# A delta-rule attention and two MoE layers on one core: the first triangular inverse cut into blocks of 16, a second room for step 1, and a new order of the program

## The chip, the cores and the metric

The kernel runs on one core of a Trainium2 chip. The metric is the device time of one execution in microseconds (us), from the first to the last instruction with the small frame around it; lower is better.

The engines by the names of the profile: PE is TensorE (matmuls; PEld its weight loads), DVE is VectorE, ACT is ScalarE, POOL is GpSimd, SP is SyncE, which here issues nearly all DMAs. Each engine works through its own instructions strictly in the order of the program; engines wait for each other by semaphores.

## The reference

Inputs are q, k, v of 4 batches x 8 heads x 768 tokens x 48 and a beta for each token. Cut to what matters:

```python
# attention: a state of 48x48 per head, updated token by token (delta rule)
k_n = k / (norm(k) + 1e-6)
for t in range(768):
    y[t]  = q[t] @ state
    state = state + beta[t] * outer(k_n[t], v[t] - k_n[t] @ state)
# first MoE-like layer: x is y as 3072 tokens x 384
h = x @ w_in                      # 384 -> 2048
x = (h * sigmoid(h)) @ w_out      # 2048 -> 384
# second: 8 experts, soft routing P by 8 rounds of row and column scaling
P = balance(exp(x @ w_gate))
out = sum over e of P[:, e] * (relu(x @ w1[e]) @ w2[e])   # 384 -> 1024 -> 384
```

w_in and w_out arrive as 64-bit floats; the kernel splits them on the chip into a high and a low 32-bit part.

## The kernel before, in words

**Attention in 12 steps of 64 tokens.** The recurrence inside a step is replaced by the inverse of a 64x64 unit lower triangular matrix per head (32 heads, in two groups `bp` of 16). `gram_k` / `gram_kq` compute the products of the keys on PE (psum `gk`, `gkq`), they are written to DRAM (`nd`) and read back by `units` so that 128 small 32x32 triangles (2 steps x 2 halves x 32 heads) lie one per partition in the tile `nu`. `tri(j, prio)` inverts these 128 triangles for the steps 2j and 2j+1 on DVE: square roots and scales (`root_act`, `d_`), a scale of `nu`, then for each of 31 columns `t` a multiply (L607, into `tmpu`) and an add (L605, into `tu`), and a last scale of `tu` (L620, kept as `O["td2", j]`). In `tri(0)` most columns are cut into two row ranges, so that two chains of instructions alternate. ACT copies `tu` into `nu` with the two inner axes turned (L623); SP writes `nu` to DRAM as `rd` (L628) and `tu` as `td` (L637).

**Step s.** `rt_load(s)` reads `rd` into the tile `rt` (L647) and `td` and `nd` into the tile `td11`. There is one `rt` and one `td11` for all steps, so the loads of step s wait until step s-1 has used them (`O["u1", s-1, bp]`, `O["z1", s-1]`, `O["r1", s-1]`). `merge(s)` joins the two 32-blocks of each head into the 64-block: 64 small matmuls (`z`, L665), two ACT evacuations (L671), 64 matmuls (`r`, L678), two ACT evacuations (L686). Then, for both `bp`: `state_read` (PE `c`, from step 1 on, then DVE `wq`, L702), `update` (PE `d`, L716, two ACT evacuations), `output` (PE `y` and `s`, and the DVE add of `s` to the state `xs`, L752) and `turn` (PE transposes `t`, ACT and DVE writing `x`, the input of the first MoE layer).

**First MoE layer.** Six blocks of two steps; block b needs the turns of steps 2b and 2b+1. For each of 16 slices f of the hidden layer there is `moe_h` (9 matmuls, L791, then ACT sigmoid, DVE multiply L801, ACT, POOL) and `moe_o` (9 matmuls, L833). They are issued between the attention steps of later blocks.

**Weight sets.** `weight` turns w_in and w_out into two parts: one load (L920), two ACT copies and seven DVE operations (L945 to L956). There are 8 sets `p` of two slices (w_in and w_out); set p is loaded into the place where set p+1 will be built. These DVE operations run before and during block 0, between all other DVE work.

**Second layer.** 64 units of 15 products (L1264) and 12 outputs (L1352), from about 690 us to the end.

**Order of the program.** Nothing is scheduled at run time. Each piece of work is added with `op(engine, cost, fn, deps, prio, ...)`; `Order.emit` is a list planner that runs once, when the program is built. It keeps an estimated time of each engine and of the DMA queue, takes at each step the piece that can start first (within a small window `NEAR` the one with the highest priority) and so fixes the order of each engine's instructions. Priorities are the `prio` arguments plus a table `NUDGE`; `ALT` is a bonus for alternating between two kinds of PE work. Before the first `moe_h` the planner fills idle PE time with dummy matmuls (`idle`, psum `idle`, L1454).

Of the kernel before, what the change touches and what calls it, by code (L numbers as in the profile page):

```python
# [10 lines left out]
F32 = mybir.dt.float32  # L11
# [3 lines left out]
AF = mybir.ActivationFunctionType  # L15
# [26 lines left out]
ALT = 12.4  # L42
# [4 lines left out]
NEAR_PE = 0.14  # L47
NEAR_DVE = 0.0
NEAR_ACT = 0.25
NEAR_POOL = 0.19  # L50

NUDGE = {
    ('ACT', '<lambda>', -15.5): -9.0, ('ACT', '<lambda>', -7.5): -4.8, ('ACT', '<lambda>', 20): 2.1, ('ACT', 'adma', 30): 3.1,
    ('ACT', 'gram_k.ev', 30): 6.7, ('ACT', 'gram_kq', 4.5): 0.1, ('ACT', 'merge', 0.5): 5.5, ('ACT', 'merge', 16): 2.6, ('ACT', 'merge', 2): -2.7,
    ('ACT', 'merge', 20.5): 1.5, ('ACT', 'merge', 22): -0.7, ('ACT', 'merge', 36): -1.8, ('ACT', 'merge', 5.5): 0.9, ('ACT', 'merge', 7): -2.1,
    ('ACT', 'moe_h.hi', 12): -6.7, ('ACT', 'moe_h.sig', 29.5): -0.8, ('ACT', 'norms.sq', -11): 1.0, ('ACT', 'output.ev', 13): 0.8,
    ('ACT', 'outputs', 4.5): 2.0, ('ACT', 'products.evac', 2): 9.1, ('ACT', 'root_act', 4): -11.5, ('ACT', 'rt_load', 32.5): -7.0,
    ('ACT', 'sinkhorn', 3.5): 0.1, ('ACT', 'step_out.cp', -3.5): 12.6, ('ACT', 'step_out.hi', 20): 3.4, ('ACT', 'tokens.parts', -3.5): 0.7,
    ('ACT', 'tri', 15.5): 3.4, ('ACT', 'turn.hi', 15): 0.1, ('ACT', 'units.go', 20): -3.3, ('ACT', 'update', 9): -1.2,
    ('ACT', 'weight.absolute', -4): -1.9, ('ACT', 'weight.hi', 7.5): 1.4, ('ACT', 'weights.hi', -0.5): 1.3, ('DVE', '<lambda>', 17.5): -5.6,  # L60
    ('DVE', '<lambda>', 40): -0.6, ('DVE', 'gram_k.ev', 30): 1.1, ('DVE', 'gram_q', 31): 0.3, ('DVE', 'mask_q', 6): 9.8,
    ('DVE', 'moe_h.mul', 18): 0.5, ('DVE', 'norms', 11): -6.1, ('DVE', 'output.add', 8): 7.6, ('DVE', 'outputs', 4.5): 21.1,
    ('DVE', 'products.add', -3.5): 16.4, ('DVE', 'root_act', 5): 1.1, ('DVE', 'root_act', 8): 4.0, ('DVE', 'root_act.fin', 5): -0.4,
# [22 lines left out]
}  # L86

TINY_HI = float(np.uint32(0x38000000).view(np.float32))


# [1412 lines left out]
```

## Time and profile before

| what | value |
|---|---|
| time, median of 3 runs | 2177.32 us (2176.47 to 2178.69) |
| the profiled execution's own time | 2183.14 us |
| span of that execution, first to last instruction | 2181.3 us |
| PE busy | 2148.3 us, 98% of the span |
| DVE busy | 1741.8 us, 80% |
| POOL busy | 1539.6 us, 71% |
| ACT busy | 1021.5 us, 47% |

The profile shows one execution. A share of busy time is an average over stages that have different limits, and a busy PE can still be at half clock or running dummy matmuls, so each stage is read by itself. [...] The DMA share is the mean busy share of the core's 16 DMA engines.

### The profile page before, as it was taken

The numbers are of one execution on the slowest core, as the hardware profiler recorded it, in microseconds if no ns is written. First come the engines' busy times: TensorE is split into PE (matmuls) and PEld (weight loads), VectorE is DVE, ScalarE is ACT, GpSimd is POOL, SyncE is SP. The second block draws the span as 40 slices with busy tenths as digits, with TensorE's granted clock in tenths as the row PEclk, the third lists the DMA queues.
The fourth block names the chain that finished last, engine by engine and source line by source line (L and its number), as shares of the span: only waits on it lengthen the run. The fifth ranks groups of instructions, "written<-read, shape, count | busy, mean of one in ns | idle before, by whom it ended". The sixth has DMA issues, their size and how long they took to land.

```text
span 2181.3 us, 40538 instructions
## 1 busy us (share of the span) xinstructions
PE 2148.3 (98%) x15814; PEld 1912.0 (88%) x15814; DVE 1741.8 (80%) x2999; ACT 1021.5 (47%) x1766; POOL 1539.6 (71%) x1387
## 2 busy tenths in 40 slices
PE   8999999999999999999999999999999999999999
PEld 7888888887877889999999999989999999999998
DVE  6888757557445988888888888888888888888887
ACT  2445343433444554545445445555444454454443
POOL 0143555645376988987888878878888878888784
PEclk9899999999999999999999999999999999999999
DMA  8876342533221101011111110120111101101111
GB/s 248 205 216 158 86 94 62 120 49 89 45 81 73 37 30 37 31 40 33 37 31 36 37 37 31 36 66 30 37 37 37 36 30 37 37 30 37 37 33 48
DMA packets 127424, 136.79 MB, mean 63 GB/s; under 512 B 83392, under 2 KB 91328, under 8 KB 127232
## 3 DMA queue, kind: packets, MB, share of 16 engines
q1 hardware_dynamic: 124864, 133.55, 21.9%
q8 instruction: 124, 2.03, 0.4%
q10 hardware_dynamic: 2368, 0.66, 0.2%
q14 instruction: 68, 0.56, 0.1%
HBM read 108.47 MB, written 25.69 MB: 62 GB/s over the span
## 4 chain that ended last, share of the span: by engine, by line
PE 82%; DVE 6%; DMA 5%; POOL 3%; ACT 1%; SPq 1%; issue 1%; DVEq 0%; POOLq 0%; ACTq 0%
PE o L1352 36%; PE p L1264 29%; PE x2p L833 5%; PE h L791 4%; PE d L716 1%; DVE s L1073 1%; DMA kqp<-gd 1%; PE gkq L456 1%; DMA ke<-in_kq 1%; DVE tmpu L607 1%; PE idle L1454 1%; PE y L731 1%; POOL g L809 1%; DVE tu L605 1%; DVE sg L801 1%
## 5 line engine op out<-in xcount | busy, mean ns | idle before, releaser
L1352 PE MATMUL o<-wb,room 128*128 128x384 f32 x2784 | 792.2, 337 | 3.9 <-POOL room L1073 2.4
L1264 PE MATMUL p<-room,wa 128*128 128x512 f32 x2880 | 732.4, 395 | 0.7 <-DVE x L856 0.7
L1264 PEld LDWEIGHTS p<-room,wa 128*128 128x128 f32 x2880 | 536.7, 189 | 92.9 <-DVE x L856 0.8
L1352 PE MATMUL o<-wb,h 128*128 128x384 f32 x1824 | 609.5, 336 | 0.2 <-ACT room L1212 0.2
L1073 DVE TENSOR_TENSOR s<-s,p 128x512 f32<-128x512 f32 x704 | 477.3, 684 | 92.7 <-PE p L1264 55.9
L1352 PEld LDWEIGHTS o<-wb,room 128*128 128x128 f32 x2784 | 512.3, 188 | 26.2 <-POOL room L1073 3.0
L1368 DVE SCALAR_TENSOR_TENSOR acc<-o,pr,acc 128x384 f32<-128x384 f32 x708 | 429.1, 614 | 83.2 <-PE o L1352 82.9
L1073 POOL TENSOR_TENSOR room<-s,room 128x512 fp32r<-128x512 f32 x232 | 305.6, 1320 | 152.9 <-ACT s L1298 146.7
L1073 POOL TENSOR_TENSOR wa<-wraw,wa 128x640 fp32r<-128x640 f32 x189 | 319.5, 1691 | 52.4 <-ACT wa L1167 50.0
L1352 PEld LDWEIGHTS o<-wb,h 128*128 128x128 f32 x1824 | 342.8, 188 | 14.1 <-ACT s L1298 0.6
L1073 POOL TENSOR_TENSOR wraw<-wraw 128x256 f32<-128x256 f32 x378 | 284.5, 761 | 11.2 <-DMA wraw<-in_w 1.9
L809 POOL TENSOR_TENSOR g<-sg,g 128x512 fp32r<-128x512 f32 x96 | 132.8, 1383 | 209.2 <-ACT g L805 197.4
L1167 ACT ACTIVATE wa<-wraw 128x640 fp32r<-128x640 f32 x189 | 138.9, 735 | 244.0 <-POOL wraw L1073 132.6
L1298 ACT ACTIVATE s<-s 128x512 f32<-128x512 f32 x384 | 242.3, 631 | 10.3
L1073 DVE TENSOR_TENSOR s<-p,s 128x512 f32<-128x512 f32 x320 | 220.2, 689 | 16.9 <-PE p L1264 2.5
L1296 ACT ACTIVATE room<-s 128x512 fp32r<-128x512 f32 x232 | 145.1, 625 | 180.2 <-DVE s L1073 178.7
L1073 POOL TENSOR_TENSOR h<-s,h 128x512 fp32r<-128x512 f32 x152 | 205.8, 1354 | 30.7 <-ACT s L1298 29.4
L833 PE MATMUL x2p<-g,w 128*128 128x512 f32 x864 | 219.2, 402 | 4.2 <-ACT g L805 2.6
L791 PE MATMUL h<-x,w 128*128 128x512 f32 x864 | 211.0, 395 | 0.6 <-DVE sg L801 0.6
L833 PEld LDWEIGHTS x2p<-g,w 128*128 128x128 f32 x864 | 160.1, 191 | 44.7 <-POOL g L809 6.2
L791 PEld LDWEIGHTS h<-x,w 128*128 128x128 f32 x864 | 159.6, 188 | 35.0 <-DVE sg L801 1.5
L1073 DVE TENSOR_TENSOR s<-s,s 128x512 f32<-128x512 f32 x192 | 173.2, 902 | 2.8
(177 smaller groups left out, 2211.4 us busy)
## 6 DMA issues: line engine op xcount, KB each, us to landing
wraw<-in_w SPq DMA_DIRECT2D x126, 384.0 KB, 2.9
kv<-in_kv SPq DMA_DIRECT2D x12, 768.0 KB, 6.0
ke<-in_kq SPq DMA_DIRECT2D x40, 192.0 KB, 4.3
kqp<-in_kq SPq DMA_DIRECT2D x40, 192.0 KB, 4.0
nd<-ke SPq DMA_DIRECT2D x20, 256.0 KB, 3.5
gd<-ke SPq DMA_DIRECT2D x20, 256.0 KB, 3.7
kqp<-gd SPq DMA_DIRECT2D x40, 128.0 KB, 4.7
wr<-in_w_in SPq DMA_DIRECT2D x6, 768.0 KB, 6.4
```

The lines of the kernel that those rows point to most:

```text
L456: nc.tensor.matmul(out=ps[0:64, h], lhsT=t[64:112, 0, h], rhs=t[64:112, k, h], start=True, stop=True)
L605: nc.vector.tensor_tensor(out=tu[:, a:b, 0:k], in0=tu[:, a:b, 0:k], in1=tv, op=ALU.add)
L791: nc.tensor.matmul(out=ps.rearrange("p (s t) -> p s t", s=2), lhsT=w[:, k, wl], rhs=X1[:, at, k, xl], start=n == 0, stop=n == 8)
L809: nc.gpsimd.tensor_tensor(out=g[:, 1], in0=T["sg", b, f], in1=f32(g)[:, 0], op=ALU.subtract)
L833: nc.tensor.matmul(out=T["x2p", b][j], lhsT=w[:, wl, 128 * j:128 * j + 128], rhs=g[:, gl], start=f == 0 and n == 0, stop=f == NF - 1 and n ...
L1073: e.tensor_tensor(out=out, in0=in0, in1=in1, op=o)
L1167: nc.scalar.activation(P2[key][:, :, 0], R(3 + 5 * g, 8 + 5 * g), AF.Copy)
L1264: nc.tensor.matmul(out=ps, lhsT=w[:, i, wl], rhs=x[:, xl], start=k == 0, stop=k == 2)
L1296: nc.scalar.activation(P2[key][:, 0], buf(x), AF.Relu)
L1298: op2("ACT", 0.52, lambda: nc.scalar.activation(buf(x), buf(x), AF.Relu), writes=[("s", n, x)], prio=PR_H)
L1352: nc.tensor.matmul(out=ps, lhsT=h[:, hl, 128 * i:128 * i + 128], rhs=w[:, wl], start=c == 0, stop=c == 5)
L1368: op2("DVE", 0.53, lambda A=A, pk=pk, t=t: nc.vector.scalar_tensor_tensor(out=A(), in0=P2[pk], scalar=P2["pr"][:, t, e:e + 1], in1=A(), op ...
```

## The change

- `tri(0)` now ends in a new function `tri_half`: it inverts only the two diagonal 16x16 blocks of each 32x32 triangle (15 columns, two independent chains on DVE), and both off-diagonal 16-blocks of `nu` are wiped by POOL. `tri(1)` to `tri(5)` stay as they were.
- For the steps 0 and 1 a new function `merge_half` joins the 16-blocks to 32-blocks on PE (64, 32 and 64+32 small matmuls), with evacuations on ACT and DVE, ahead of the old `merge`. `td` of these steps is stored and loaded in other pieces; `z` of these steps reads `gneg` in SBUF where it read `nd` through `td11`, so a buffer of `gneg` is kept until `z` is done.
- Step 1 has its own `rt` and `td11` (`RT[1]`, `TD[1]`), in the place of weight set `NP - 2` (`spare`). So the weight set `NP - 3`, whose load goes to that place, waits for step 1's `update` (`O["u1", 1, bp]`), and the last three weight sets are added after step 1.
- The rule for the dummy matmuls is new: `need` counts the columns that PE has done in the last stretch and asks for up to 14 dummies ahead of an operation that waits; a gap is filled from 0.32 us where it was 0.5 us.
- Costs and landing times of the DMAs in the planner are new, `NUDGE` is new (a value can now count for the first n pieces of a kind only, and each piece can have its own window `hold`), `ALT` is 14.4 where it was 12.4, and the windows `NEAR` of PE, ACT and POOL change. For the kinds of work of the second layer the priorities of the main run of units keep their values, but for the output stores.

```diff
-ALT = 12.4
+ALT = 14.4
-NEAR_PE = 0.14
+NEAR_PE = 0.0
-NEAR_ACT = 0.25
-NEAR_POOL = 0.19
+NEAR_ACT = 0.4
+NEAR_POOL = 0.33
 NUDGE = {
...
-    ('DVE', 'weight', 1.5): -5.0,
+    ('DVE', 'weight', 1.5): (-0.9, -6.0, 55, 0.07),
...
+GAP, WARM = 0.32, 1052.0
...
+    def need(self, t, at, cost, cols):
+
+        unit = 1.0 if self.fast(max(0, int((t - self.PHASE) / self.TICK + 1 + 1e-6))) else 1.85
+        for f in range(14):
+            since = max(t + f * 0.107 * unit, at) + cost * unit - self.TICK
+            done = 0.0
+            for a, b, c in reversed(self.did):
+                if b <= since:
+                    break
+                done += c * (b - max(a, since)) / (b - a)
+            if done + 80 * f + cols >= WARM:
+                return f, unit
+        return 14, unit
...
-                    while idle and not busy and t > IDLE and now[e] + 0.5 < t:
-                        order.append((now[e], len(order), None))
+                    fill = idle and not busy and t > IDLE
+                    f = self.need(now[e], r, cost, cols)[0] if fill and r > IDLE else 0
+                    while fill and (now[e] + GAP < t or f > 0):
+                        f -= 1
+                        order.append(None)
...
-    rv = rt.rearrange("p b h c -> p (b h) c")
+    spare = place(NP - 2, shape=(3 * H * CH,), dtype=F32, name="spare")
+    RT = [rt, spare[:, 0:2 * H * CH].rearrange("p (b h c) -> p b h c", b=2, h=H)]
+    TD = [td11, spare[:, 2 * H * CH:].rearrange("p (u c) -> p u c", u=16)]
+    def inv(s):
+
+        return RT[1] if s == 1 else rt, TD[1] if s == 1 else td11
...
         x = op("DVE", 1.0, d_, roots + [O["bu"]], prio=prio)
+        if j == 0:
+            return tri_half(x, fill, prio)
...
+    def tri_half(x, fill, prio):
+        sub = (slice(0, 16), slice(16, 32))
...
+        ends = [op("DVE", 0.34, lambda a=a: v.tensor_tensor(
+            out=nu[:, a, a], in0=nu[:, a, a], in1=du[:, 1, a].unsqueeze(2).to_broadcast(sh), op=ALU.mult),
+            [(x, 0.13), fill], prio=prio, port=True) for a in sub]
...
+        for t in range(15):
+            for add in (False, True):
+                for q in range(2):
+                    ends[q] = op("DVE", 0.07 + (15 - t) * (t + 1) / 960, lambda t=t, q=q, add=add: col(t, q, add),
+                                 [(ends[q], 0.13)], prio=prio, turn=1, port=True)
+        cps = []
+        for q, a in enumerate(sub):
+            x = ends[q] = op("DVE", 0.34, lambda a=a: v.tensor_tensor(
+                out=tu[:, a, a], in0=tu[:, a, a], in1=du[:, 1, a].unsqueeze(1).to_broadcast(sh), op=ALU.mult),
+                [(ends[q], 0.13)] + ([(ends[0], 0.0)] if q else []), prio=prio, port=True)
+            cps.append(op("ACT", 0.6, lambda a=a: nc.scalar.activation(nu[:, a, a].rearrange("u c r -> u r c"), tu[:, a, a], AF.Copy), [x], prio=15.5))
...
-                O["rd", j][s % 2:s % 2 + 1] + ([O["u1", s - 1, 0], O["u1", s - 1, 1]] if s else O["rt0"]), prio=12.5 + FIRST[s], lands=(1.33, 0.55) if by == "ACT" else 1.33))
+                O["rd", j][s % 2:s % 2 + 1] + ([O["u1", max(0, s - 1 - (s == 2)), bp] for bp in range(2)] if s > 1 else O["rt0"][s]),
+                prio=12.5 + FIRST[s], lands=(2.4, 0.4) if by == "ACT" else 1.9))
...
+    def merge_half(s):
...
+        a = op("PE", 1.7, z, O["rtl", s] + [w], prio=14 + FIRST[s], take=["a"], turn=1 if s else None, cols=221)
+        e = op("ACT", 0.4, lambda: nc.scalar.activation(T["y1", s][:, :, up], T["z16", s], AF.Copy), [a], prio=18 + FIRST[s])
...
+        c = op("PE", 1.0, lambda: r(1), [e] + O["tdl", s][0:2], prio=13 + FIRST[s], take=["a"], turn=1 if s else None, cols=221)
+        f = [op("ACT", 0.35, lambda o=o: nc.scalar.activation(rv[o:o + 16, :, 48:64], T["r16", s, 1][o:o + 16, 0], AF.Copy),
+                [c], prio=17 + FIRST[s]) for o in (32, 96)]
...
+        d = op("PE", 1.9, lambda: r(0), [e] + O["tdl", s][2:4], prio=11 + FIRST[s], take=["a"], turn=1 if s else None, cols=221)
...
+        g = [op("DVE", 0.35, lambda o=o: nc.vector.tensor_copy(out=rv[o:o + 16, :, up], in_=T["r16", s, 0][o:o + 16, 0]),
+                [d], prio=20 + FIRST[s]) for o in (0, 64)]
+        h = [op("DVE", 0.35, lambda o=o: nc.vector.tensor_tensor(
+            out=td11[o:o + 32, :, 0:16], in0=td11[o:o + 32, :, 0:16], in1=T["r16", s, 0][o:o + 32, 1], op=ALU.add),
+            [d], prio=21 + FIRST[s]) for o in (0, 64)]
...
-        a = O["z1", s] = op("PE", 1.13, z, O["rtl", s][:2] + O["gll", s], prio=10 + FIRST[s], take=["a", "sg"], turn=1 if s else None, cols=221)
+        a = O["z1", s] = op("PE", 1.13, z, O["rtl", s][:2] + O["gll", s] + O.get(("j22", s), []), prio=10 + FIRST[s], take=["a", "sg"], turn=1 if s else None, cols=221)
...
+        if p == NP - 3:
+            free = free + [O["u1", 1, 0], O["u1", 1, 1]]
...
-        a = op("SP", 1.08 * m, ld, free, prio=-9 if n >= 4 else 9.2)
+        a = op("SP", (1.3 if kind else 0.9) * m, ld, free, prio=-9 if n >= 4 else 9.2, lands=2.5)
...
+        if s == 1:
+            for p in range(NP - 3, NP):
+                weight_set(p)
```

## Rows read from the trace of the kernel before

**Rows 1.** Page: the span.

```profile
span 2181.3 us, 40538 instructions
```

**Rows 2.** Stretches: busy of PE, PEld, DVE, ACT, POOL (instructions); PEclk; DMA share; GB/s.

```profile
10.80:121.80 111.00, 98.79 (x1787) 94.43 (x1787) 86.82 (x246) 43.28 (x74) 11.95 (x11) 0.83 0.83 219
...
121.80:208.00 86.20, 85.35 (x1115) 70.04 (x1112) 79.56 (x169) 45.62 (x77) 28.36 (x24) 1.00 0.71 199
720.00:2160.00 1440.00, 1434.90 (x7293) 1309.91 (x7292) 1250.43 (x1975) 715.70 (x1218) 1200.68 (x1067) 1.00 0.11 35
```

**Rows 3.** Stretches of 10 us ahead of the first MoE matmul, same columns.

```profile
50.00:60.00 10.00, 8.13 (x87) 7.92 (x84) 9.97 (x37) 4.52 (x6) 0.00 (x0) 0.83 1.04 363
80.00:90.00 10.00, 10.00 (x182) 9.31 (x180) 5.87 (x14) 5.67 (x11) 1.07 (x1) 0.50 0.90 243
110.00:120.00 10.00, 8.67 (x158) 7.76 (x155) 3.95 (x8) 3.67 (x8) 3.75 (x3) 0.55 0.60 168
```

**Rows 4.** Chain that ended last, in time: start us, us, what.

```profile
37.89 9.18 DMA ke<-in_kq
...
81.08 1.84 PE z L665 x64
...
89.21 3.11 PE d L716 x64
...
100.48 1.13 PE z L665 x64
...
108.16 2.59 PE d L716 x48
...
121.89 2.26 PE h L791 x9
...
193.20 0.55 DVE wt L948
```

**Rows 5.** Timeline of DVE: start us, us, engine, line, operation, shapes [idle before it].

```profile
23.29 0.19 DVE L531 TENSOR_SCALAR rta<-nu 128x32 f32<-128x32 f32 x1 [1.54 <-DMA td<-nd]
...
27.00 0.27 DVE L607 TENSOR_TENSOR tmpu<-nu,tu 128x16 f32<-128x16 f32 x2
27.21 0.27 DVE L605 TENSOR_TENSOR tu<-tu,tmpu 128x16 f32<-128x16 f32 x2
...
30.68 0.42 DVE L607 TENSOR_TENSOR tmpu<-nu,tu 128x72 f32<-128x72 f32 x2
31.01 0.42 DVE L605 TENSOR_TENSOR tu<-tu,tmpu 128x72 f32<-128x72 f32 x2
...
43.56 0.56 DVE L945 TENSOR_SCALAR wt<-wt 128x768 f32<-128x768 f32 x1 [4.81 <-ACT wt L924]
...
63.50 1.22 DVE L620 TENSOR_TENSOR tu<-tu,du 128x1024 f32<-128x1024 f32 x1
...
103.34 0.54 DVE L702 TENSOR_TENSOR wq<-kv,c 128x384 f32<-128x384 f32 x1
...
207.47 0.56 DVE L956 SCALAR_TENSOR_TENSOR w<-wr 128x384 fp32r<-128x384 uint32 x1
```

**Rows 6.** Groups of DVE instructions up to 121.8 us: count | busy us, mean ns.

```profile
L607 DVE TENSOR_TENSOR tmpu<-nu,tu 128x120 f32<-128x120 f32 (+40 forms) x59 | 13.5, 253 | 0.2
L605 DVE TENSOR_TENSOR tu<-tu,tmpu 128x120 f32<-128x120 f32 (+40 forms) x59 | 12.7, 254 | 0.0
```

**Rows 7.** Timelines of ACT and of SP's queue, columns as in rows 5.

```profile
68.82 1.98 ACT L623 ACTIVATE nu<-tu 128x1024 f32<-128x1024 f32 x1
...
92.35 2.65 SPq L647 DMA_DIRECT2D rt<-rd  x4
...
106.30 1.20 ACT L686 ACTIVATE rt<-r 32x512 f32<-32x512 f32 x2 [1.58 <-PE r L678]
```

**Rows 8.** DMA issues: engine, count, KB each, median us to landing.

```profile
rd<-nu SPq DMA_DIRECT2D x12, 256.0 KB, 3.1
rt<-rd SPq DMA_DIRECT2D x46, 64.0 KB, 2.6
```

More of the change, by code (lines that the diff above doesn't have):

```diff
@@ new lines @@
+    ('ACT', 'products.hidden.hi', 5.5): (-0.0, -2.7, 14), ('ACT', 'root_act', 4): (-7.4, 0.0, 0, 0.54), ('ACT', 'rt_load', 32.5): (0.2, 0.0, 0, 0.38),
+    ('ACT', 'sinkhorn', 3.5): (0.1,), ('ACT', 'step_out.cp', -3.5): (0.3,), ('ACT', 'step_out.hi', 20): (-0.1, 0.0, 0, 0.46),
+    ('ACT', 'tokens.parts', -3.5): (0.7,), ('ACT', 'tri', 15.5): (-0.4, 0.0, 0, 0.4), ('ACT', 'turn.hi', 15): (0.8, 11.7, 4, 0.05),
+    ('ACT', 'units.go', 20): (-0.3, 0.0, 0, 0.69), ('ACT', 'update', 9): (-4.1, -7.2, 8, 0.34), ('ACT', 'weight.absolute', -4): (-5.4, 0.6, 11, 0.29),
@@ L197, in emit @@
                     if r is not None:
-                        lane = lanes[-8] + 0.1 if e in self.QUEUES and len(lanes) >= 8 else 0.0
+                        lane = lanes[-8] + 0.1 if (e in self.QUEUES or self.ops[i][9]) and len(lanes) >= 8 else 0.0
                         r = max(r, now[e])
+                        if e == "PE" and idle and not busy and r > IDLE:
+                            free = max(now[e], IDLE)
+                            f, unit = self.need(free, r, self.ops[i][1], self.ops[i][7])
+                            lane = free + f * 0.107 * unit
                         c.append((max(r, lane, port["POOL" if e == "DVE" else "DVE"] if self.ops[i][8] else 0.0), i, r))
@@ L208, in emit @@
                 t0 = min(c)[0]
-                t, i, r = min((x for x in c if x[0] <= t0 + self.NEAR[e]), key=rank)
+                t, i, r = min((x for x in c if x[0] <= t0 + self.NEAR[e] + self.hold[x[1]]), key=rank)
                 if best is None or (t, r) < best[:2]:
                     best = (t, r, i, e)
-            t, _, i, e = best
+            t, r, i, e = best
             left[e].remove(i)
@@ L661, in z, with low @@
+    def merge(s):
+        rv, td11 = rows(inv(s)[0]), inv(s)[1]
+        if s < 2:
+            merge_half(s)
+        def low(o, u):
+            return T["gneg", s].rearrange("p b h c -> p (b h) c")[o + 32:o + 64, u, 0:32] if s < 2 else td11[o + 32:o + 64, u]
         def z():
@@ L664, in z @@
                 for o in (0, 64):
-                    nc.tensor.matmul(out=ps[o:o + 32, u], lhsT=td11[o + 32:o + 64, u],
+                    nc.tensor.matmul(out=ps[o:o + 32, u], lhsT=low(o, u),
                                      rhs=rv[o + 32:o + 64, u, 32:64], start=True, stop=True)
@@ L1007, with weight_set @@
         out=wgr[:, :, 1], in0=wgs, in1=f32(wgr)[:, :, 0], op=ALU.subtract), [x], prio=0)
-    for p in range(NP):
+    def weight_set(p):
         for kind in range(2):
@@ L1011 @@
                 weight(kind, f, 2 if p < NP - 2 else 1)
+    for p in range(NP - 3):
+        weight_set(p)
     for s in range(2):
```

171 lines of the change are left out of this document (128 added, 43 removed), and 33 rows, old and new, of the table NUDGE.

## Prediction

> **What bounds the kernel now.** I read the stretches first. From 121.80 us on PE is busy nearly without a break at full clock: 85.35 of 86.20 us up to 208 us, 1434.90 of 1440 in the second layer, granted 1.00 [rows 2]. Ahead of that, from 10.80 us, 98.79 of 111.00 us look busy, but this is not useful work: the mean grant is 0.83, and a good part is dummies. So the time is a lead of 121.89 us, where the first matmul of the first MoE layer starts [rows 4], plus about 2059 us of dense PE work. The change takes nothing out of the second part; it pays by as much as the lead gets shorter, as long as PE then still finds work.
>
> What sets the lead I read from the timeline of DVE and the chain. Three pieces follow each other. (A) The first inverse: its scales start at 23.29 us, columns at 27.00, the last scale ends at 63.50 + 1.22 = 64.72: 41.4 us [rows 5]. (B) From there to the first `update` at 89.21: 24.5 us for the copy, store, load and merge [rows 4, 7]. (C) From 89.21 to 121.89: 32.7 us for steps 0 and 1 [rows 4].
>
> A second limit runs beside it. DVE also splits the MoE weights; the last of those ends at 207.47 + 0.56 = 208.0 us [rows 5], and in block 0 the chain passes through such a piece at 193.20 us [rows 4]. From 121.80 to 208 us DVE is busy 79.56 of 86.20 us [rows 2]. So block 0 has PE and DVE nearly full at once.
>
> **Part A, blocks of 16.** Two column instructions of 16 elements each (with their partner of the other chain) take 27.21 - 27.00 = 0.21 us, two around 72 (the partner about 105) take 31.01 - 30.68 = 0.33 us [rows 5]: about 0.096 us per instruction plus 0.73 ns per element. Before, 59 multiplies and 59 adds [rows 6] over 2 x 5456 elements make 118 x 0.096 + 10912 x 0.00073 = 19.3 us. Of the 36.5 us between 27.00 and 63.50 another 4.8 us are a stall of DVE behind a weight piece whose load came late [rows 5]; the other 12 us are weight pieces put in between. After: 15 columns x 2 x 2 = 60 instructions over 2720 elements, 60 x 0.096 + 2720 x 0.00073 = 7.7 us. The scale before and the one after, 1.22 us each for 1024 elements [rows 5], become two of 256 each, 0.7 us together. Roots and factors stay at about 2.4 us. Sum: 2.4 + 0.7 + 7.7 + 0.7 = 11.5, ending at 34.8. No weight piece was put in before 38 us in the old run, because their loads had not landed; I allow one, so 36: **28.7 us less, taken as 28** (24 with six pieces in between, 30 with none and faster scales). POOL's two wipes lie beside this.
>
> [...]
>
> **Part B, the join.** New on the path: `z16`, an evacuation, half of `r16`, two evacuations. The nearest row is `z`, 64 matmuls with 32 columns: 1.13 us at full clock, 1.84 at half [rows 4]. `z16` has 64 with 16 columns: 0.57 (half) to 1.84; I take 1.13, the nearest row in count. The first `r16` has 32: 0.57. An evacuation pair of 32x512 takes 1.20 us [rows 7]; the new ones have half the elements, so 0.3 to 1.2 each; I take 0.6 and 1.0. The whole path: last copy 0.6 (half of the old 1.98 overlaps, the rest is a quarter more), store 3.1, load 2.6 + three issues ahead of it 2.0 [rows 7, 8], 1.13, 0.6, 0.57, 1.0, then `z` 1.13, 1.2, `r` 1.13, 1.2, and some 1.4 of hand-overs: 17.7 us. The same sum without the new pieces and with the 1.98 copy is 15.4 for the old path, which took 24.5: 9 us were waits (the copy starts only at 68.82, four us after the tile is ready [rows 7]; half clock costs 0.7 us on `z` [rows 4], 0.50 granted in 80 to 90 us [rows 3]). I expect two thirds of these waits again: 24.2, so **no gain or loss in B** (from -6.7 without any wait to +12.7 where the DMAs are late, see the second rival). The other half of `r16` and its four DVE writes are needed only before `r`, beside `z`; if DVE takes them late, `r` waits up to the length of a weight piece, 0.6 us.
>
> [...]
>
> Queues: per pair of steps SP issues 2 `td` stores where it issued 4, the rest is equal in number; `gneg` is held until `z`, and the hidden layer needs that buffer only 10 us later. The four DVE writes per step at about 0.54 us (a PSUM read of 384 elements, [rows 5]; 256 here, so 0.3 to 0.54) add up to 3.8 us on DVE for two steps.
>
> **Part C, the second room.** Step 1's four loads are issued at 92.35, after step 0's `update` [rows 7]; its `z` runs at 100.48 [rows 4], its last evacuations start at 106.30 [rows 7], its `update` at 108.16 [rows 4], although the second `wq` is there at 103.34 + 0.54 = 103.9 [rows 5]. With its own room all of this can lie beside step 0, and `update` follows `wq`: 4 us earlier at the start, and at full clock its end comes at about 105 where it came at 112.8: 8 us. Another 2 us come from the clock, which was at 0.55 between 110 and 120 us [rows 3]. **C: -10 us** (-13 to -5). The new dummies cost something in return: up to 14 ahead of a waiting operation; I take 2 us for the path (0 to 5). The head, before 23.29 us, changes only through the new order: -1 (-5 to +2), and I leave it out against rounding.
>
> **First MoE matmul:** 121.9 - 28 - 10 + 2 = about 85 to 86 us, 37 us earlier (24 to 45).
>
> **What block 0 gives back.** DVE's work from 10.8 us, where the first weights are there, to the last weight piece is 86.82 + 79.56 = 166.4 us [rows 2]. Removed: 19.3 - 7.7 and about 1.1 of scales; added: the 3.8 of PSUM writes; so 157.5. Its idle time was 111.0 - 86.8 = 24.2 us up to 121.8 and 6.6 from there to 208. The 24.2 shrink with the lead to 24.2 x (85 - 10.8) / 111 = 16.2; the 6.6 stay. So the last weights come at 10.8 + 157.5 + 16.2 + 6.6 = 191, only 17 us earlier. Block 0 ends between the two: 17 us earlier if DVE alone rules, 37 if PE can fill with other work (key products, steps 2 and 3). DVE is on the chain there today [rows 4], but PE never starved, so I take the middle: **27 us**. The late load of weight set `NP - 3` costs nothing by itself: it waits for step 1's `update`, some 40 us of PE work before its slice comes up.
>
> After block 0 nothing changes in work. In the second layer PE idles 5.1 of 1440 us [rows 2]; the new order can neither win nor, if the priorities of its main run hold, lose much.
>
> **Sum.** Profiled execution 2183.1 (span 2181.3 [rows 1] and 1.8 around it) - 27 = 2156. The median of the runs, 2177.3, is 5.8 below that execution, so the forecast in its terms is **2150 us**.
>
> **Rivals.** (1) *PE fills block 0 completely*: all 37 us arrive: 2140. For it: 85.35 of 86.20 us PE busy although DVE was at 92% [rows 2]. Against it: DVE's sum above. (2) *The chain waits for DMAs instead.* The store and loads after the inverse move from 71 us to about 37 to 45, into the stretch in which bulk loads run: the DMA share is 1.04 between 50 and 60 us [rows 3], and a load issued at 37.89 took 9.18 us [rows 4]. If each leg takes that, it costs 9.2 - 3.1 and 9.2 - 2.6: 12.7 us; the first MoE matmul comes at 98, DVE idles 3 us more, and between 15 and 24 us are left, with later loads crowded too rather 15: 2162. (3) *The change shortens the inverse, but the start doesn't move*: DVE, in strict order, waits for weight loads as at 43.56 (4.81 us) [rows 5] more often, since there is less else to do. Then 9.4 us less work turn into idle time and the last weights come at 208: 2177, no change. (4) *Slower, in the second layer.* `ALT` 14.4 and `NEAR` 0 for PE reorder all 64 units. Today a unit loses 5.1 / 64 = 0.08 us of PE. If a product is placed ahead of its operand in each unit and PE waits 0.5 us or more, 64 x 0.5 = 32 us eat the gain of 27 and the measurement's uncertainty; at 0.55 us: 2185. Against it: the priorities there keep their values.
>
> **How the numbers follow.** Forecast (own range 2143 to 2157) 0.50; PE fills 0.13; DMAs 0.22; no change 0.07; slower 0.08. A measurement can tell 0.2%, 4.4 us, from no change. Faster: 0.50 + 0.13 + 0.22 = 0.85; same 0.07; slower 0.08. The range goes from the second case with B's best bound, 2140 - 6, to the DMA case with 8 us of further waits: 2134 to 2170; it leaves out cases 3 and 4 and a little of each other one.
>
> **What would show it.** Right: 60 column instructions on DVE, the last scale near 36 us; loads of step 1 issued before step 0's `update`; first MoE matmul at 80 to 92 us; last weight piece at 185 to 195; PE idle below 8 us in the second layer. Wrong: store or load legs of 6 us and more (case 2), DVE idle in one piece before weight operations (case 3), granted clock still at 0.5 in the merges (B and C lose 4 us), PE waits of half a microsecond in each unit (case 4).

## The result: 1% slower, and the profile after

The changed kernel takes 2198.5 us (median) where the kernel before takes 2176.9 beside it: ratio 1.0101, 95% interval 1.0082 to 1.0119, 21.6 us more. The forecast was 27 us less.

The page of the changed kernel (span), then three stretches of it with the columns of rows 2 (PEclk is the granted clock as a share of full speed): the lead up to the first `h` matmul, block 0, the second layer.

```profile
span 2197.4 us, 41741 instructions
```

```profile
10.80:129.60 118.80, 106.10 (x2212) 101.11 (x2210) 77.16 (x201) 38.63 (x71) 12.85 (x16) 0.74 0.71 183
129.60:216.00 86.40, 86.11 (x1167) 69.86 (x1164) 72.64 (x152) 46.48 (x78) 29.25 (x26) 1.00 0.68 184
728.00:2176.00 1448.00, 1441.11 (x7326) 1313.11 (x7325) 1258.00 (x1987) 727.39 (x1227) 1217.76 (x1072) 1.00 0.11 35
```

Against rows 1 the profiled span is 16.1 us longer. Against rows 2: the lead ends at 129.6 where it ended at 121.8, with DVE 10 us *less* busy (77.16 against 86.82) and the clock at 0.74 instead of 0.83. The second layer is as dense as before (6.9 us of 1448 without PE; from its first `p` matmul to its last `o` matmul 1490.4 us, before 1490.3), so nothing was lost there. The rest of the 16.1 us, 8.3, arises between the first `h` and the first `p`. Work that was put off comes to as much. These are the key products (columns as above) in the lead of the changed kernel; before there were 608 of them, 22.97 us:

```profile
10.80:129.60 118.80, 11.95 (x288) 11.11 (x288) 5.25 (x9) 0.74 0.71 183
```

320 products at 0.033 us (64 of them take 2.1 us behind the first `h`) are 10.5 us of PE that now lie behind it, against 64 read products (2.1 us) that were drawn forward. So the first `h` at 129.6 even flatters the change.

Where the lead went is told by the chain that ended last, in order of time (start, length, what; "issue" is time in which the engine waited for nothing that the profile shows, `idle` are the fillers, called dummies in the prediction):

```profile
19.38 0.21 ACT nident L1170
19.63 15.79 PE idle L1632 x120
...
39.29 5.01 PE idle L1632 x43
...
48.18 10.39 PE idle L1632 x91
...
63.42 2.01 issue
...
73.06 2.22 PE idle L1632 x9
...
79.79 0.97 issue
...
81.26 2.22 PE idle L1632 x9
...
85.53 1.15 issue
...
87.52 2.43 PE idle L1632 x10
...
91.81 1.27 issue
...
94.17 2.22 PE idle L1632 x9
...
102.39 3.03 PE d L886 x58
...
109.14 4.64 PE idle L1632 x24
```

and by the timelines of DVE and ACT (columns of rows 5):

```profile
33.69 0.42 DVE L731 TENSOR_TENSOR tu<-tu,du 128x256 f32<-128x256 f32 x1
```

```profile
39.34 0.60 ACT L532 ACTIVATE ke<-gkq 128x512 f32<-128x512 f32 x1 [0.34 <-PE gkq L517]
39.84 1.08 ACT L734 ACTIVATE nu<-tu 128x256 f32<-128x256 f32 x2
```

The inverse is done at 34.1 us, 30.6 earlier than in rows 5. But ACT copies it only at 39.84, because ahead of that in its order stand four copies of key products, which PE could not start before 35.4: it was working off 120 fillers that had themselves waited for `nident` until 19.6. `z16` runs at 62.2, the first `d` at 101.8. In two stretches, columns as above:

```profile
34.00:64.00 30.00, 29.42 (x608) 28.82 (x607) 18.71 (x38) 10.95 (x21) 3.95 (x4) 1.00 0.68 196
64.00:111.90 47.90, 43.08 (x1024) 40.41 (x1024) 25.45 (x48) 16.31 (x29) 1.89 (x2) 0.51 0.62 155
```

PE looks 98 and 90% busy in them, DVE 62 and 53%. In the second the granted clock is at the lower of the two levels in the trace (0.50; the other is 1.00) almost throughout; it fell at 65.0, within the 2.01 us stop that begins at 63.42.

### The profile page after: what moved, and what is told of

The parts are those of the page before. It is cut to its first block, busy times and chain, and to the rows that moved or that the text cites. A ratio compares the mean times of both kernels' runs of the same rounds, so it can differ in the third digit from the quotient of the medians.

```text
span 2197.4 us, 41741 instructions
## 1 busy us (share of the span) xinstructions
PE 2166.1 (99%) x16466; PEld 1926.0 (88%) x16466; DVE 1733.0 (79%) x2951; ACT 1028.4 (47%) x1773; POOL 1550.2 (71%) x1393
## 3 DMA queue, kind: packets, MB, share of 16 engines
q1 hardware_dynamic: 123872, 133.61, 21.6%
q8 instruction: 129, 2.11, 0.4%
## 4 chain that ended last, share of the span: by engine, by line
PE 91%; DVE 5%; DMA 2%; ACT 1%; issue 1%; POOL 0%; SPq 0%; DVEq 0%; ACTq 0%; POOLq 0%
PE o L1530 35%; PE p L1442 28%; PE h L962 8%; PE x2p L1004 8%; PE idle L1632 2%; DVE s L1251 2%; PE gkq L516 2%; PE d L886 1%; PE y L902 1%; PE c L867 1%; PE z L833 1%; PE r L846 1%; PE s L918 1%; DVE acc L1546 1%; DVE room L1251 0%
## 5 line engine op out<-in xcount | busy, mean ns | idle before, releaser
L1251 POOL TENSOR_TENSOR wa<-wraw,wa 128x640 fp32r<-128x640 f32 x189 | 298.4, 1579 | 110.7 <-ACT wa L1345 110.7
L1251 POOL TENSOR_TENSOR wraw<-wraw 128x256 f32<-128x256 f32 x378 | 309.3, 825 | 7.8 <-DMA wraw<-in_w 1.9
L980 POOL TENSOR_TENSOR g<-sg,g 128x512 fp32r<-128x512 f32 x96 | 129.6, 1351 | 218.7 <-ACT g L976 210.2
L1251 POOL TENSOR_TENSOR h<-s,h 128x512 fp32r<-128x512 f32 x152 | 210.7, 1387 | 42.4 <-ACT s L1476 42.4
L1251 DVE TENSOR_TENSOR s<-p,s 128x512 f32<-128x512 f32 x320 | 219.7, 687 | 25.6 <-PE p L1442 11.7
L962 PE MATMUL h<-x,w 128*128 128x512 f32 x864 | 220.5, 404 | 0.6 <-DVE sg L972 0.6
L1004 PEld LDWEIGHTS x2p<-g,w 128*128 128x128 f32 x864 | 159.9, 189 | 35.8 <-ACT g L976 1.3
L1251 DVE TENSOR_TENSOR s<-s,s 128x512 f32<-128x512 f32 x192 | 183.7, 957 | 2.6
L972 DVE TENSOR_TENSOR sg<-h,sg 128x512 f32<-128x512 f32 x96 | 66.2, 690 | 145.4 <-ACT sg L968 142.5
```

Source lines behind the costliest of these rows:

```text
L962: nc.tensor.matmul(out=ps.rearrange("p (s t) -> p s t", s=2), lhsT=w[:, k, wl], rhs=X1[:, at, k, xl], start=n == 0, stop=n == 8)
L972: nc.vector.tensor_tensor(out=sg, in0=T["h", b, f], in1=sg, op=ALU.mult)
L980: nc.gpsimd.tensor_tensor(out=g[:, 1], in0=T["sg", b, f], in1=f32(g)[:, 0], op=ALU.subtract)
L1004: nc.tensor.matmul(out=T["x2p", b][j], lhsT=w[:, wl, 128 * j:128 * j + 128], rhs=g[:, gl], start=f == 0 and n == 0, stop=f == NF - 1 and n ...
L1251: e.tensor_tensor(out=out, in0=in0, in1=in1, op=o)
```

## The experiments

Each change of a single thing starts from the changed kernel ("after") or, from e6 on mostly, from the run without fillers (e2). Read from the timelines of PE: the first key product, the first join product `z16`, the time from there to the first `d` of step 0, and the first `h`.

| run | first key product | z16 | z16 to d | first h | median us | ratio to before |
|---|---|---|---|---|---|---|
| before | 27.2 | - | - | 121.8 | 2177 | 1 |
| after | 35.3 | 62.2 | 39.6 | 129.6 | 2198.5 | 1.0101 (1.0082 to 1.0119) |
| e1 operand | 25.4 | 54.3 | 41.1 | 120.8 | 2189.2 | 1.0057 (1.0029 to 1.0084) |
| e2 no fillers | 22.4 | 52.7 | 35.0 | 117.0 | 2182.2 | 1.0021 (0.9999 to 1.0043) |
| e3 none in merges | 36.6 | 63.4 | 35.8 | 126.0 | 2191.2 | 1.0058 (1.0037 to 1.0079) |
| e4 before, no fillers | 23.4 | - | - | 117.5 | 2178.0 | 0.9999 (0.9988 to 1.0010) |
| e5 whole blocks | 34.6 | - | - | 135.3 | 2213.6 | 1.0141 (1.0085 to 1.0196) |
| e6 half the joins | 23.2 | 52.9 | 25.0 | 109.4 | 2175.6 | 0.9996 (0.9974 to 1.0018) |
| e7 weights held | 23.3 | 53.4 | 35.8 | 125.0 | 2210.1 | 1.0149 (1.0111 to 1.0186) |
| e8 more weights held, rd first | 24.0 | 48.4 | 29.9 | 116.7 | 2237.5 | 1.0275 (1.0235 to 1.0314) |
| e9 nu held | 24.3 | 54.1 | 33.0 | 127.7 | 2203.1 | 1.0113 (1.0085 to 1.0141) |
| e10 nu held, early fillers | 25.2 | 52.9 | 32.5 | 126.0 | 2205.8 | 1.0114 (1.0094 to 1.0134) |
| e11 early fillers | 25.3 | 52.3 | 37.1 | 118.7 | 2185.7 | 1.0029 (1.0013 to 1.0045) |
| e12 old rule | 24.8 | 53.3 | 21.2 | 123.3 | 2193.7 | 1.0063 (1.0044 to 1.0082) |
| e13 short weight loads | 23.9 | 53.9 | 29.6 | 108.1 | 2178.4 | 1.0006 (0.9992 to 1.0019) |
| e14 four loads held | 23.1 | 53.3 | 33.1 | 124.4 | 2205.1 | 1.0132 (1.0110 to 1.0154) |
| e16 early fillers, short loads | 28.4 | 55.2 | 29.7 | 109.3 | 2178.8 | 1.0015 (0.9998 to 1.0032) |
| e17 one room | 24.2 | 54.2 | 23.0 | 134.8 | 2219.9 | 1.0203 (1.0176 to 1.0231) |

### First question: fillers, clock, loads, or the blocks themselves?

**e1**, a constant as the fillers' operand:

```diff
-    x = op("DVE", 0.2, lambda: nc.vector.memset(tmpu[:, 0:128], 0.0), prio=40)
+    x = op("DVE", 0.2, lambda: nc.vector.memset(tmpu[:, 0:128], 0.5), prio=40)
-    O["nident"] = op("ACT", 0.2, lambda: nc.scalar.activation(nident, ident, AF.Copy, scale=-1.0), ...
+    O["nident"] = op("ACT", 0.2, lambda: None, ...
```

> The fillers multiply a constant that DVE writes at the very start, so that none of them waits for the copy that ACT makes of the identity at 19.28; the plan and the order are those of the changed kernel. Left out: that copy. Theory W (the fillers stand in PE's order ahead of the small products, begin late and hold them up): the 120 fillers that now fill 19.63 to 35.42 run from about 10 on, the key products start near 27 rather than at 35.35, the copy of the inverse follows the last scale at about 35 rather than 39.84, the first z16 at about 54 rather than 62.16, the first h product near 121, 2190 us. Theory K (the half clock from 64 to 112 is the loss, the fillers only fill waits): the same start of the key products as W, but the merges still take about 40 us and the first h product is at 125 or later. Theory L (the loads of the product operands land late whatever PE does): z16 stays within 2 us of 62.16 and h within 2 us of 129.6.

The key products start 9.9 us earlier, `z16` 7.8, the first `h` 8.9 and the median falls by 9.3 us: theory W for that part, and L falls. The merges are no shorter (41.1 us), and the clock is at its lower level in them as before (0.50 from 60 to 95 us).

**e2**, no filler emitted (the plan still has them, so the order is the same):

```diff
             if i is None:
-                idle()
+                continue
```

> The changed kernel in the same order, with no filler emitted at all (359 fewer matmuls on PE). Left out: fillers only. Theory W: key products at about 23, z16 at about 50, the merges up to the first d (39.6 us in the changed kernel) at 20 to 25, the first d near 73 and the first h product at 100 to 108; about 2175 us. Theory K: without fillers the clock is at its half from the start to the first MoE product, the merges take 39.6 us or more, and the first h product comes at 125 to 135. Theory L: z16 at about 60, the merges shorter by the fillers among them (some 12 us), h at about 118 to 125.

16.3 us less than after: three quarters of the loss is fillers. But the first `h` is at 117.0, not 100 to 108, and `z16` to `d` still takes 35.0 us. Neither W alone nor K: the clock is at the lower level (0.50) from 35 to 110 us, and all the same everything comes earlier than with fillers. Its chain, as above:

```profile
35.62 7.20 DMA rd<-nu
42.84 7.40 DMA rt<-rd
...
63.37 1.37 issue
...
67.42 4.86 issue
...
75.02 4.21 issue
...
82.15 1.28 issue
...
88.29 3.03 PE d L886 x58
```

Two legs through DRAM take 7.2 and 7.4 us. And PE stands four times, 11.7 us in all, with nothing to wait for, in the middle of products that have started. Counted in the trace, 1710, 1965, 2220 and 2475 matmuls and weight loads had begun at these four points: 255 apart, and 256 apart (1729, 1985, 2241, 2497) with the semaphore records of PE's sequencer. The stops within a product or a run of fillers in the kernel before (1217, 3265, 3521) and in after (1729, 2497, 2753, 3009, the first of them the 2.01 us stop among the fillers) leave the same remainder, 193, when these counts are divided by 256. The traced transfers also hold packets of 16 KB in a queue of their own, named instruction in the list of DMA queues of that stretch (52 to 90 us; packets, MB, share of 16 engines):

```profile
q8 instruction: 8, 0.13, 1.7%
```

Four of them end at 63.20, 70.67, 77.81 and 81.98; PE goes on at 64.74, 72.27, 79.23 and 83.43, 1.4 to 1.6 us behind each. Theory S of the later runs reads this as PE out of instructions until the next packet has come; so far that is an inference from these counts and times.

**e3**, no fillers from the first `z16` on:

```diff
+        at = min(order.index(i) for i, o in enumerate(self.ops) if "merge_half" in o[2].__qualname__ and o[0] == "PE")
-        for i in order:
+        for n, i in enumerate(order):
             if i is None:
-                idle()
+                if n < at:
+                    idle()
```

> The changed kernel in the same order; the fillers ahead of the first z16 stay, those from it on are left out. All theories: z16 within 1 us of 62.16. Theory W: from z16 to the first d 20 to 25 us rather than 39.6, since 8 to 10 fillers of 0.23 us stood ahead of nearly every small product; the first h product at about 112, 2182 us. Theory K: the clock stays at the half, and the products and copies between z16 and d take 34 us or more; h at 124 or later. Theory L: in between, as each product waits for a copy or a load behind which the fillers stood: 28 to 34 us, h at 118 to 124.

```profile
76.79 4.54 issue
...
84.07 4.28 issue
...
91.18 2.08 issue
```

The chain of e3: 12.8 us of fillers fewer between `z16` and `d` (seven groups of 0.7 to 2.4 us in after), and the merges are only 3.8 us shorter, because the stops grew from 1.0, 1.2 and 1.3 us (after) to 4.5, 4.3 and 2.1. So the fillers in the merges mostly filled time in which PE, without them, stands in these stops: theory W's 15 to 20 us fall here.

**e5**, the first inverse over whole blocks again:

```diff
-        if j == 0:
-            return tri_half(x, fill, prio)
...
-        if s < 2:
+        if False:
             return res, [], [op("SP", 0.4, lambda ab=ab, h=h: nc.sync.dma_start(
...
-        if s < 2:
-            merge_half(s)
```

> The changed kernel with one part undone: the first inverse runs over whole blocks of 32 again (DVE), without the joins on PE; second room, filler rule and priorities are the new ones. If the blocks of 16 and their joins are what costs (they stand on the path with PE at half clock), the first h product comes earlier than in the changed kernel, at 118 to 124, and the time is 2180 to 2188. If the blocks of 16 give what they should (28 us of DVE) and the new order and fillers are what costs, the first h product moves to 140 to 150 and the time to 2205 to 2220. If neither, 2195 to 2200.

First `h` 5.7 us later and 15.1 us more in the median than after: the blocks of 16 do help, though by less than the 10 to 20 us at the first `h` that their 28 us of DVE would give. The planner ordered the rest anew around this edit (640 key products ahead of the first `h` where after has 288, 490 fillers instead of 359), so this is the blocks together with the order that goes with them, not the blocks alone.

**e4**, the kernel before without fillers (edit as in e2):

> The kernel before, in its own order, with no filler emitted (347 fewer matmuls). Left out: fillers only. If fillers cost in the old order what they cost in the new one (17 us of the span there), the first h product comes at 105 to 112 rather than 121.82 and the time is about 2160 to 2168. If the old rule placed them in time that PE waits anyway, h stays within 3 us of 121.82, or comes later by what the half clock costs (2178 to 2190).

First `h` 4.3 us earlier, time unchanged. In the old order fillers cost nothing in the end; in the new one they cost 16.3 us. And with fillers out of both, old and new order reach the first `h` at the same time, 117.5 and 117.0, and the new one still has 320 key products to do then: the 28 us of the inverse are all spent elsewhere in the lead.

**e11**, the edits of e1 and e3 together:

> The changed kernel in its order, with the two edits on the fillers together: constant operand (the copy on ACT left out), and none from the first z16 on. If both act by themselves, the 8.9 us that the first gave at the first h product and the 3.6 of the second add up: h at 117, 2184 us. If PE's supply of instructions sets the joins, they don't: z16 to the first d stays at 35 to 37 us, h at 116 to 119, as without any filler (116.98), though the clock is at its full level until z16 rather than until 35.

118.7 and 2185.7 us: like no fillers at all. The clock at its upper level (1.00) until 57 us brought nothing.

**e12**, the filler rule of before in the new order, constant operand:

```diff
-                            lane = free + f * 0.107 * unit
+                            lane = 0.0
...
-                    while fill and (now[e] + GAP < t or f > 0):
+                    while fill and now[e] + 0.5 < t:
```

> The changed kernel with the filler rule of the kernel before (fill any wait over 0.5 us, no running sum, products not held back for it) and the constant operand; blocks of 16, second room and priorities are the new ones. If the new rule is what costs beside the operand (7 of 17 us), the first h product comes at 112 to 118 and the time is 2180 to 2184. If it is fillers of any rule in this order, h at 119 to 122 and 2187 to 2191, as with the constant operand alone.

2193.7 us, above both bands. With the old rule the changed kernel is no faster than with the new one and the same operand (e1, 2189.2). That the rule alone costs nothing isn't shown by this, as the planner made another order with it: the first `d` begins at 74.5 here, but step 1's joins moved behind it, and `h` to 123.3.

### Second question: do PE's stops come from its instructions?

**e6**, half of the joins, no fillers:

```diff
-            for u in range(16):
+            for u in range(8):
...
-        e = op("ACT", 0.4, lambda: nc.scalar.activation(T["y1", s][:, :, up], T["z16", s], AF.Copy), ...
+        e = op("ACT", 0.4, lambda: nc.scalar.activation(T["y1", s][:, 0:8, up], T["z16", s][:, 0:8], AF.Copy), ...
```

in both products of `merge_half`, and in its other copies likewise.

> The run without fillers, with the products of the joins (z16, r16) and their copies over 8 of the 16 units only: 320 of 640 matmuls, and as many weight loads, are left out. Order, loads and all the rest stay. In the run without fillers z16 to the first d took 35.0 us (52.69 to 87.7), of which PE stood 11.8 us with nothing to wait for that the profile shows, in four stops that lie 255 matmuls and weight loads apart. Theory S (PE stops for its own instructions, which come in packets of 16 KB beside the data transfers): 640 instructions fewer are two and a half packets fewer, each worth up to 7 us from stop to stop: z16 to d 20 to 26 us. Theory K (the small products at half clock are the time): 320 matmuls of some 0.017 us, 5.5 us less: 29 to 30 us. Theory D (the path waits for copies and loads, not for PE): within 2 us of 35.

25.0 us, in the band of S (20 to 26) and below that of K and D: 640 instructions fewer, with copies of half the size, are worth 10.0 us, nearly twice the 5.5 us at which K puts their work.

**e7**, weights held:

```diff
+        O.setdefault("wlds", []).append(len(sc.ops))
         a = op("SP", (1.3 if kind else 0.9) * m, ld, free, prio=-9 if n >= 4 else 9.2, lands=2.5)
...
+    for i in O["wlds"][5:10]:
+        sc.ops[i][3].append((O["r1", 1], None))
```

> The run without fillers, with the sixth to tenth load of MoE weights (768 KB each, issued from 61 to 77 there) held until the last product of the second inverse's merge; the planner orders the rest anew around that. No work is left out but the fillers. Theory S: with 3.8 MB fewer on the DMA queues between 60 and 95 the stops of PE every 255 instructions shrink from 1.4, 4.9, 4.2 and 1.3 us to 1.5 us or less each, and z16 to the first d takes 24 to 28 us rather than 35.0; the first h product at 106 to 110 if its weights are there. Theory K: the stops go but the products stay at the half clock: 32 to 35 us. Theory D: copies on ACT no longer stand behind the weights' magnitudes: 28 to 32 us, with the stops still there.

The four stops, counted as pauses between two starts of more than 0.9 us, went from 1.6, 5.1, 4.4 and 1.5 us to 2.4, 2.3, none and 1.2. But the time to `d` stayed at 35.8, since the planner put 102 more key products between (6.5 us more of them), and the first `h` came 8 us later: S in the stops, no gain. As the order moved, e13 was needed.

Two more runs held weight loads, both without fillers: **e8** the third to tenth load, with rd stored ahead of td, and **e14** the seventh to tenth load until step 0's `r` only. Neither computes what the kernel computes, though no work was to be left out but the fillers (why stays open), so of their times only the stops say something. These went the way of e7: 1.6, 1.4, 1.4 and 2.3 us in e8, and 1.6, 2.3 and 3.1 in e14. The forecasts for the rest missed: e14's first `h` came at 124.4 where 109 to 114 was expected and its time is 2205.1, not 2172 to 2180; e8's first `h` came at 116.7 where 105 to 115 was expected.

**e13**, the same five loads cut to 1/32 in an unchanged order:

```diff
+            few = 48 if call in range(5, 10) else m * DM
+            if few < m * DM:
+                nc.gpsimd.memset(f32(T[key])[:, few:], 0.0)
-            nc.sync.dma_start(out=T[key], in_=src[:, f:f + m].bitcast(I32).rearrange("p f (c w) -> p (f c) w", w=2))
+            nc.sync.dma_start(out=T[key][:, 0:few], in_=src[:, f:f + m].bitcast(I32).rearrange("p f (c w) -> p (f c) w", w=2)[:, 0:few])
```

> The run without fillers in exactly its order, but of the sixth to tenth MoE weight load only 48 of 1536 columns are fetched (24 KB of 768), and the rest is set to zero on POOL: the weights of five loads are left out. Theory S (PE stops at every 255th matmul or weight load until its next packet of instructions has come past the data transfers): the stops of 1.4, 4.9, 4.2 and 1.3 us shrink to 0 to 2.4 each as with the weights held, and z16 to the first d takes 27 to 30 us rather than 35.0 with the same products in the same order; the first h product at 108 to 111. Theory T (the stops are PE's own, for instance from its small products, whatever moves on the queues): stops and the 35 us stay.

The chain of e13:

```profile
64.69 1.65 issue
...
69.02 1.56 issue
...
73.33 2.29 issue
...
78.54 0.73 issue
...
108.20 2.28 PE h L962 x9
```

The same stops at the same instructions, 6.2 us instead of 11.7; 29.6 us to `d` instead of 35.0; the first `h` 8.8 us earlier. The stretch from 65 to 80 us, first without fillers (e2), then in e13 (columns as above, the last two the DMA share and GB/s):

```profile
65.00:80.00 15.00, 5.46 (x289) 5.13 (x283) 6.32 (x12) 4.63 (x7) 0.83 (x1) 0.50 1.04 287
```

```profile
65.00:80.00 15.00, 8.60 (x411) 8.14 (x413) 11.25 (x20) 5.04 (x9) 4.54 (x4) 0.50 0.69 124
```

With fewer bytes on the queues PE gets 411 matmuls done instead of 289. That is what theory S expected, and T falls. What is left of the stops (1.6 us in the mean) is there without the weights. Of the 8.8 us only 3.9 reach the median, and in the two profiled executions none (spans of 2180.1 and 2181.5 us). A part is lost again behind the first `h`: between 300 and 720 us the granted clock is 1.00 in e2 (first line) and 0.97 in e13; what let it fall there stays open.

```profile
300.00:720.00 420.00, 413.79 (x4164) 341.72 (x4160) 253.49 (x468) 174.62 (x325) 240.81 (x225) 1.00 0.28 73
```

```profile
300.00:720.00 420.00, 414.23 (x3995) 341.83 (x3994) 243.69 (x452) 171.29 (x318) 232.94 (x218) 0.97 0.26 70
```

**e16**, e11 with the same short loads:

> The run with early fillers only (constant operand, none from z16 on), with the same five weight loads cut to 24 KB. Theory S: as there, and if the clock is still at its full level when the joins run (it fell after a stop in every run before), they take 18 to 23 us, h at 102 to 106. If the clock falls all the same at the first short wait: 27 to 31 us, h at 109 to 113. Theory T: 36 to 37 us, h at 117 to 119.

29.7 us, `h` at 109.3: S again, and the clock falls all the same. It was at the upper level up to 60.9 us, two us past the first stop (1.99 us from 56.88), and the joins took as long as at half clock throughout (e13).

**e9** and **e10**, other transfers kept out of the joins (rd stored first, nu loads held until step 0's `r`), without fillers and with early ones:

```diff
+    for i in O["nl", 1]:
+        sc.ops[i][3].append((O["r1", 0], None))
...
-            O["td", 0].append(op("SP", 0.95, lambda i=i: w_td(64 * i), [x] + [(y, -9.0) for y in O["td", 0]], ...
+            O["td", 0].append(op("SP", 0.95, lambda i=i: w_td(64 * i), [x] + cps + [(O["rd", 0][0], -9.0)] + [(y, -9.0) for y in O["td", 0]], ...
```

> No fillers; the store of rd ahead of that of td, and the eight loads of the second inverse's input (nu from nd, issued from 58 to 61 and from 73 to 77 in the run without fillers) held until step 0's last merge product. Weights where they were; no work is left out but the fillers. Theory S (PE stops for its own instructions, and the stops are as long as the DMA queues are full): z16 at 48 to 49 rather than 52.69, z16 to the first d 28 to 31 us rather than 35.0, the first h product at 107 to 111 rather than 116.98, and 2172 to 2177 us if the MoE blocks behind don't take it back. Theory D (loads and copies, not PE's supply): z16 at 48 to 49 as well, z16 to d still 34 to 36 us, h at 112 to 113.

> The run with early fillers only, with rd stored first and the eight nu loads held as above. Theory S: z16 at 50 to 52, z16 to d 28 to 31 us, h at 108 to 113, 2174 to 2180 us. Theory D: z16 to d 34 to 36 us, h at 113 to 116.

Both missed: 33.0 and 32.5 us to `d`, and `z16` no earlier. The weight loads stayed where they were (DMA share 0.92 to 1.07 from 65 to 80 us in e9), and so did stops of 4.3 and 5.6 us. Step 1's merge slid behind step 0, and the first `h` to 126 to 128: a hold that looks free moves the whole order.

### Third question: what is the second room worth?

**e17**, one room, no fillers:

```diff
-        return RT[1] if s == 1 else rt, TD[1] if s == 1 else td11
+        return rt, td11
...
-                O["rd", j][s % 2:s % 2 + 1] + ([O["u1", max(0, s - 1 - (s == 2)), bp] for bp in range(2)] if s > 1 else O["rt0"][s]),
+                O["rd", j][s % 2:s % 2 + 1] + ([O["u1", s - 1, bp] for bp in range(2)] if s else O["rt0"][s]),
...
-                O["td", 0][s:s + 1], prio=11.5 + FIRST[s], ...
+                O["td", 0][s:s + 1] + ([O["z1", 0], O["r1", 0]] if s else []), prio=11.5 + FIRST[s], ...
```

> The run without fillers with the second room for step 1's product operands taken away again: step 1's loads of rt go to the one room and wait until step 0's u products have read it, those of td until step 0's merge product has. No work is left out but the fillers. If the second room is worth the 10 us that the prediction gave it, the first h product comes at 125 to 129 rather than 116.98 and the time is 2186 to 2192. If PE's supply and the half clock set that stretch (step 0's first d to the first h took 29.3 us without fillers), the room is worth 0 to 5 us: h at 114 to 122, 2180 to 2186.

```profile
134.84 3.35 PE h L962 x9
```

17.8 us at the first `h` and 37.6 in the median: far more than either band. A part of it is the new order that the planner made (416 key products ahead of `h` instead of 288), and the 20 us behind the first `h` stay open. At the same time `z16` to `d` of step 0 is 12.0 us *shorter* (23.0 against 35.0), because step 1's joins and its `z`, 384 matmul records, no longer stand in between; the key products there are as many as before (91 and 90). Both are true of the room: step 1 goes beside step 0, and step 0 pays for it with PE's instructions.

No variant that leaves no work out but fillers beats the kernel before; the best with the change in it, e2, is 0.2% above it (interval from 0 to 0.4%).

## Why the prediction was wrong, point by point

**Part A held.** Last scale at 34.1 (34.8 to 36 forecast), 60 column instructions between 25.82 and 33.65, 7.8 us where the sum said 7.7. The gain, 30.6 us, lies just above the 24 to 30 given, as no weight piece was put in between. (The rows of the sum give about 0.82 ns per element, not 0.73; for the 60 instructions this moves the sum by less than 0.1 us.)

**Part B failed, at the sentence "I expect two thirds of these waits again: 24.2".** From the last scale to the first `d` it took 67.7 us, and 53.8 without fillers. The working of the 17.7 us priced each product by its work and put the rest as waits like the old ones. (By its own terms the old path adds up to 15.7, not 15.4, and the forecast to 23.6, not 24.2; beside the miss this is small.) What the runs show in place of that, for the 29.6 us above 24.2 in e2: step 1's joins, which I had beside the path, stand ahead of step 0's `d`, 12.0 us (e17); the two DRAM legs took 7.2 and 7.4 where I took 3.1 and 2.6, 8.9 us; the rest, 8.7 us, is half clock, hand-overs and the stops that e17 has too (3.9 us in one piece); I can't split it further. The stops, 11.7 us in e2, cut across these: 5.5 of them come from the five weight loads (e13). The trace of before had them already, as its chain shows; I took them for hand-overs and did not count instructions:

```profile
51.19 1.87 issue
...
104.11 0.97 issue
...
110.75 1.33 issue
```

The joins add 320 matmul records per step (of `z` there are now 384 ahead of the first `h` where there were 128, of `r` 512 where there were 128) with as many weight loads: 1280 records in two steps, five times the 255 that lie between two stops of e2. "The nearest row in count" was wrong too. `z`, given above as 64 matmuls, is 32 in the program, and the x64 of its row are records, two per matmul; `z16` has 64 matmuls and 128 records, and the joins of a step have 64, 32 and 32 + 32 matmuls. The price still held: at half clock `z16` took 1.83 us and the old `z` 1.84. What the miscount hid is that the joins bring twice the instructions for that time.

**The term for the dummies failed: 2 us (0 to 5); they cost 16.3.** 9.3 of it is the operand (e1): the fillers stood behind one ACT copy, that behind a late weight piece, and the key products, the ACT copy of the inverse and its store behind the fillers. I named this kind of queue for the late half of `r16` and not for the fillers, whose rule and operand stood in the diff. With the old rule in place of the running sum the time is no better (e12), though in another order.

**Part C was mis-sized both ways.** The stretch from `d` to `h` shrank by 4.8 us (32.7 to 27.9) where I had 10, as it ran at half clock up to 112.8 and held 24 fillers of 4.64 us. Without the room and with the order that the planner then makes, the first `h` comes 17.8 us later (e17), although 12.0 us are saved in B.

**Block 0** was not put to the test by the change, as the lead did not get shorter. e13 gives a hint: its first `h` comes 13.7 us ahead of that of the kernel before (108.1 and 121.8), but its second layer begins no earlier (first `p` at 687.4 in both). By the rows above, 8.4 us of that are the key products put off, less the read products drawn forward; the rest stays open. That all key products would stay ahead of the first `h` I took for granted; 320 moved behind it.

**The rivals.** The second, late DMAs, was right in its mechanism (legs above 6 us, as the list at the end asked for) and roughly in size (8.9 us against 12.7), but it is the smaller part. The fourth put the risk of a slower kernel into the second layer, where nothing changed, and gave it 0.08. The third assumed that DVE waits before weight pieces: from 34 to 110 us in after it did so for 5.0 us, behind ACT's first copy of the piece, and for longer in other work (7.2 us in one wait for ACT, 4.0 and 3.0 for the joins on PE). (Its 9.4 us of less work are 8.9 by the terms of the sum.) No rival had fillers or PE's instructions, and so the range ended at 2170.

## What to carry to other kernels

Count instructions, not only work: where an engine runs hundreds of small matmuls in a few microseconds, look for stops in the middle of a product at equal counts (in e2 four, 255 records apart, 11.7 us), and see what moves on the DMA queues at that time (five loads cut to 1/32 in e13: 6.2 us). A filler in a strict order can cost what other work costs (16.3 us in the new order, nothing in the old one): ask what its operand waits for and what stands behind it. What is taken from one engine in a lead is worth only what the next leg lets through, so sum the legs with the durations of the stretch into which they move.

## What the hardware showed

**In e2 PE's stops in the joins lie 255 matmuls and weight loads apart, and 1.4 to 1.6 us ahead of the end of each a packet of 16 KB ends in the queue named instruction.** In the whole of after that queue moved 129 packets (2.11 MB), and PE has 32932 records of matmuls and weight loads, 129.1 times 255; in before it is 124 packets (2.03 MB) and 31628 records, 124.0 times 255. `z16` of step 1 in after works off 256 records in 1.83 us at half clock. Around the stops of after named above four packets end at 64.07, 79.56, 85.24 and 91.59, and PE goes on at 65.43, 80.76, 86.68 and 93.08, 1.2 to 1.5 us behind each. The list of the queues gives instruction and data as shares of the same 16 DMA engines: 1.7% and 76.3% in e2 from 52 to 90 us. From 64 to 82 us the instruction queue moved three packets beside 4.78 MB of data in e2, and four beside 1.99 MB with the weights held (e7). The four ends given for e2 are 7.5, 7.1 and 4.2 us apart, at a DMA share of 1.04 from 65 to 80 us. That PE waits for the packet is an inference from these counts and times; what the runs show is the stops going from 11.7 to 6.2 us as five weight loads shrink to 24 KB (e2, e13).

**In after, e11 and e16 the granted clock fell from 1.00 to 0.50 in a stop of PE of about 2 us, or up to two us behind it.** In after it was low from 65.0 to 112.8 us, although PE was busy 44 of 48 us; it rose within one unbroken run of 24 fillers (109.1 to 113.8 us). With fillers ahead of the joins it stayed at 1.00 only until the first stop or two us past it (e11: stop of 2.27 us at 53.99, fall at 56.9; e16: 1.99 us at 56.88, fall at 60.9).
